# Near products over blocks of 8 in the fifth step, whole bursts and more unread matmuls in the first step of an RWKV-6 and MoE kernel

## The chip, the core and the metric

The kernel runs on one core of a Trainium2 chip. The metric is the device time of an execution in microseconds (us); lower is better. The kernel before was measured at 631.83 us (median of 3; 630.54 to 633.44). Engines: PE (TensorE, matmuls; PEld its weight loads), DVE (VectorE), ACT (ScalarE), POOL (GpSimd), SP (issues DMA).

## The reference

```python
# attention: B=4, H=8, S=768, D=48; per head a D x D state
for t in range(S):
    cur = einsum('bhd,bhe->bhde', u[None] * kt, vt)
    y[:, :, t] = einsum('bhd,bhde->bhe', rt, state + cur)
    state = wt[:, :, :, None] * state + einsum('bhd,bhe->bhde', kt, vt)
# then, on x = y as (3072 tokens, 384):
h = x @ w_in                      # 384 -> 2048
sp = softplus(h)
out = (h * erf(sp)) @ w_out       # 2048 -> 384
```

## The kernel before

Twelve steps, s = 0 to 11, each of 2 x 128 tokens. A step attends (small matmuls and DVE work); the dense layers of earlier steps are laid between as "pieces", so that PE has work while DVE prepares. Inside a half of 64 tokens the products of r and k with their decay are made level by level: blocks of 2 tokens, 4, and so on to 64. Each level is a burst of small matmuls into `pp`, then a scaling of r and k by DVE, on which the next level's burst waits. From s = DIRECT = 4 on, the first four levels are replaced: products of tokens less than 16 apart in a block of 16 are computed element by element ("near products") during the step before, so the step's bursts begin at level 5.

```python
# prepare(s), near products of a block of 16 (cut)
for n in range(1, NEARER):             # NEARER = 5: DVE does distances 0 to 4
    if s == DIRECT and n == NEARER - 1:
        yield
    term(nc.vector, n)                 # terms[n] = r[n:] * k[:16-n]
    carry(nc.vector, n + 1)            # k *= decay
for n in range(1, 4):
    sum_up(n)
for n in range(NEARER, 9):             # GpSimd does the others
    term(nc.gpsimd, n)
    carry(nc.gpsimd, n + 1)
# ... sums over d on DVE, to DRAM and back into the layout of `own`
```

In the first step there are no dense layers to fill PE. Unread matmuls (identity times zeros, results never used) are put there to keep PE's clock up:

```python
# attend(s), one level (cut)
parts = 1 if s else NJ                 # NJ = 2: in step 0 the burst comes in two halves
for part in range(parts):
    for n in range(part * JP // parts, (part + 1) * JP // parts):
        ...                            # 4 small matmuls into pp for each n
    scale(s, level, part, parts)       # DVE
    keep_busy(DM // 2)                 # s == 0 only: one unread matmul of 192 columns
```

The end of a step's attention fades the state on POOL, behind POOL's near products in its queue:

```python
if c:
    nc.gpsimd.tensor_mul(faded[0][:], S[:], ...)                       # L484
...
nc.vector.tensor_add(middle[rows(e)], faded[0][rows(e)], ps[0][...])   # L512, PE's y waits for it
```

Of the kernel before, what the change touches and what calls it, by code (L numbers as in the profile page):

```python
# [15 lines left out]
ALU = mybir.AluOpType  # L16

P = 128
EP = 64
HC = 64  # L20
NC = 2
NJ = 2
# [10 lines left out]



DIRECT = 4
NEAR_LOG = 4
NEARER = 5
NEAR = 1 << NEAR_LOG
LOG = 6  # L40
MASKED = 5


def view(ap, offset, dims):

    return bass.AP(ap.tensor, ap.offset + offset, [ap.ap[0], *dims])
# [12 lines left out]
def kernel(  # L59
# [14 lines left out]
    nc = tc.nc  # L74
    PSUM = bass.MemoryType.PSUM

    n_steps, _, _, JP, C = rkw.shape
    NH, D = v.shape[2:]
    NP = JP // NJ
    NE = NH // JP  # L80
# [51 lines left out]
    def load_step(s, parts=1):  # L132
# [13 lines left out]
        nc.sync.dma_start(out=vt[:], in_=v[s])  # L146
        loaded[s] = t, vt

    rows_of = {}

    def load_rows(s):
# [66 lines left out]
    def rows(e, n=D):  # L218
        return slice(e * EP, e * EP + n)
# [4 lines left out]

    ready = {}

    def scale(s, level, part=0, parts=1):


        in_t, tots = loaded[s][0], ready[s][1]  # L230
        half, nb = 1 << (level - 1), (JP * C >> level) // parts
        halves = view(
            in_t[:, 0:2], half + part * nb * 2 * half,
            [[JP * C - half, 2], [2 * half, nb], [1, half]],
        )
        nc.vector.tensor_mul(  # L236
            halves, halves, view(tots[level - 1], part * nb * 2, [[1, 2], [2, nb], [0, half]])
        )

    def prepare(s):  # L240


        in_t = loaded[s][0]
        if s < DIRECT:
            rk1 = att.tile([P, 2, JP, C], FP32, name="rk1", bufs=1)
            parts = 1 if s else NJ
            def multiply_u(i, x):
                n = slice(i * JP // parts, (i + 1) * JP // parts)
                with_u, plain = (
                    [  # L250
                        t[:, x, n].rearrange("p n (t two) -> p n t two", two=2)[..., one]
                        for t in (rk1, in_t)
                    ]
                    for one in (x, 1 - x)
                )
                if not s and not x:
                    nc.vector.tensor_mul(
                        with_u[0], with_u[1],
                        u_sb[:, :, None].to_broadcast([P, NP, C // 2]),
                    )  # L260
                    nc.vector.tensor_copy(out=plain[0], in_=plain[1])
                    return
                for p in range(NP):
                    of = slice(p, None, NP)
                    nc.scalar.mul(
                        out=with_u[0][:, of], in_=with_u[1][:, of], mul=u_sb[:, p : p + 1]
                    )
                nc.scalar.copy(plain[0], plain[1])

            if s < 2:  # L270
                for i in range(parts):
                    for x in range(2):
                        multiply_u(i, x)
                yield
            else:
                yield
                yield
                multiply_u(0, 0)

        tots, tot = [], in_t[:, 2].rearrange("p n t -> p (n t)")  # L280
        tot_sb = att.tile([P, JP * (C - NC)], FP32, name="tot_sb")
        used = 0
        for level in range(1, LOG + 1):
            tots.append(tot)
            nb = JP * C >> level
            new = tot_sb[:, used : used + nb]
            pair = tot.rearrange("p (n two) -> p n two", two=2)
            nc.gpsimd.tensor_mul(new, pair[:, :, 0], pair[:, :, 1])  # L288
            tot = new
            used += nb  # L290
            if level == 2 and s < DIRECT:
                yield
        if s < DIRECT:
            ready[s] = rk1, tots, tot
            yield
            if s >= 2:
                yield
                multiply_u(0, 1)
            return

        own = att.tile([P, NH, HC], FP32, name="own")
        ready[s] = own, tots, tot
        if s == DIRECT:
            yield

        r, k, w = rows_of.pop(s)
        front = att.tile([P, 2, JP, C], FP32, name="rk1", bufs=1)
        back = wide.tile([P, 2, DM, 2], I32, name="words", bufs=3)
        front = front[:].rearrange("p x n t -> p (x n t)")
        back = back[:].rearrange("p x n two -> p (x n two)").bitcast(FP32)  # L310
        terms = {}

        for room, distances in (
            (front, range(1, 4)), (back, (0, 4)), (front, range(5, 9)), (back, range(9, NEAR))
        ):
            used = 0
            for n in distances:
                size = (NEAR - n) * D
                terms[n] = room[:, used : used + size].rearrange("p (t d) -> p t d", d=D)
                used += size  # L320

        def sum_up(n):
            nc.vector.tensor_reduce(  # L323
                out=view(sums[:], n, [[NEAR + 1, NEAR - n]]), in_=terms[n],
                axis=mybir.AxisListType.X, op=ALU.add,
            )

        def carry(engine, n):

            if 1 < n < NEAR:  # L330
                engine.tensor_mul(  # L331
                    k[:, : NEAR - n], k[:, : NEAR - n], w[:, n - 1 : NEAR - 1]
                )

        def term(engine, n):
            engine.tensor_mul(terms[n], r[:, n:], k[:, : NEAR - n])  # L336

        nc.vector.tensor_mul(terms[0], k, u_row[:, None, :].to_broadcast([P, NEAR, D]))
        for n in range(1, NEARER):
            if s == DIRECT and n == NEARER - 1:  # L340
                yield
            term(nc.vector, n)
            carry(nc.vector, n + 1)
        for n in range(1, 4):
            sum_up(n)
        for n in range(NEARER, 9):
            term(nc.gpsimd, n)
            carry(nc.gpsimd, n + 1)
        if s == DIRECT:
            yield  # L350
        nc.vector.tensor_mul(terms[0], terms[0], r)
        for n in (0, 4):
            sum_up(n)
        for n in range(9, NEAR):
            term(nc.gpsimd, n)
            carry(nc.gpsimd, n + 1)
        yield
        for level in range(1, NEAR_LOG):
            scale(s, level)
        yield  # L360
        for n in range(NEARER, NEAR):
            sum_up(n)
        by_blocks = dram.tile([P, NEAR, NEAR], FP32, name="by_blocks")
        nc.sync.dma_start(out=by_blocks[:], in_=sums[:])
        by_tokens = att.tile([P, NH, NEAR], FP32, name="by_tokens", bufs=1)
        nc.sync.dma_start(
            out=by_tokens[:], in_=by_blocks[:].rearrange("(g b) s t -> (b s) g t", g=NH)
        )
        yield
        scale(s, NEAR_LOG)  # L370
        nb = HC // NEAR
        nc.vector.tensor_mul(
            own[:].rearrange("p n (b t) -> p n b t", t=NEAR),
            block_sb[:, None, :].to_broadcast([P, NH, HC]).rearrange(
                "p n (b t) -> p n b t", t=NEAR
            ),
            by_tokens[:, :, None, :].to_broadcast([P, NH, nb, NEAR]),
        )

    def attend(s, xT, place, behind):  # L380
# [26 lines left out]
                    ps[:], lhsT=ident[:], rhs=in_t[:, 2, :NP], start=True, stop=True  # L407
                )

        for level in range(NEAR_LOG + 1 if s >= DIRECT else 1, LOG + 1):  # L410
            half = 1 << (level - 1)
            rk = made[:] if level == 1 else RK

            pp = products([P, NE, JP, HC])
            m = HC if level <= MASKED else half
            parts = 1 if s else NJ
            for part in range(parts):
                for n in range(part * JP // parts, (part + 1) * JP // parts):
                    for s0 in range(0, C, HC):
                        for e in range(NE):  # L420
                            t0 = s0 if level <= MASKED else s0 + half
                            nc.tensor.matmul(  # L422
                                pp[s0 : s0 + m, e, n, :m],
                                lhsT=rk[rows(e), 1, n, s0 : s0 + m],
                                rhs=rk[rows(e), 0, n, t0 : t0 + m],
                                start=True,
                                stop=True,
                            )
                scale(s, level, part, parts)
                keep_busy(DM // 2)  # L430
            if level == 1 and s == 1:
                stay_warm()
            got = pp[:].rearrange("p e n t -> p (e n) t")
# [214 lines left out]
    def in_order(s, k):  # L648


        for what in ("APPPAPP", "APPPHH", "AHHH", "AHHH")[k]:
            if what == "A":
                advance()
            elif what == "P":
                piece(projs, s - 3)
            else:
                piece(hids, s - 1)
# [170 lines left out]
```

## Time and profile before

| what | before |
|---|---|
| median time | 631.83 us |
| the execution that was profiled | 637.18 us, span 635.4 us |
| PE, DVE, ACT, POOL busy | 97%, 65%, 47%, 44% |
| mean granted PE clock in that execution | 0.981 |

On the profile's page each digit of a row is one of 40 equal slices of the span, in tenths of busy time; in the row PEclk it is the granted clock. "L422 x64" is a group of 64 instruction records of line 422 (an fp32 matmul has two); an arrow in brackets names what ended the idle time before an instruction. Line numbers move by a few between kernels: L422 before is L423 after (the bursts), L606 is L607 (second dense layer), L500 is L501, L484 is L485.

### The profile page before, as it was taken

To read this page: it belongs to the slowest core of one execution; us is meant where nothing else is said; L and a number is where in the kernel's file an instruction comes from. 1 tells how busy PE (TensorE), PEld (TensorE's weight loads), DVE (VectorE), ACT (ScalarE), POOL (GpSimd) and SP (SyncE) were. 2 spreads that over 40 slices of the span, in tenths; PEclk is the share of its full clock that TensorE was granted. 3 is DMA by queue.
4 is the path that set the end of the run, shared out by engine and by line. 5 is a ranking of instruction groups with operands and counts; after the bars stand their busy time and mean duration, and the time that the engine had idled before them with its cause. 6 is when DMAs were issued, how large, how long until landed. Compare 5 with 4: busy or idle time off the path is not lost.

```text
span 635.4 us, 15400 instructions
## 1 busy us (share of the span) xinstructions
PE 619.3 (97%) x6822; PEld 455.2 (72%) x6822; DVE 412.9 (65%) x453; ACT 301.2 (47%) x374; POOL 278.0 (44%) x288
## 2 busy tenths in 40 slices
PE   7989999999799999999999999999999999999997
PEld 6757787578458758758758758758758758768654
DVE  5579498798896797796796797797796430020200
ACT  2446778726534552552552552552553543544600
POOL 4147265549288079079079078078079100000000
PEclk9599999999799999999999999999999999999999
DMA  8167281530600240240240240240220100000000
GB/s 333 78 225 239 103 298 58 203 102 2 200 36 21 52 176 13 63 173 13 59 177 13 69 167 21 58 170 22 44 110 12 26 13 13 7 23 3 1 25 25
DMA packets 32818, 54.82 MB, mean 86 GB/s; under 512 B 19568, under 2 KB 24944, under 8 KB 31344
## 3 DMA queue, kind: packets, MB, share of 16 engines
q1 hardware_dynamic: 31600, 53.25, 24.1%
q8 instruction: 53, 0.87, 0.5%
q10 hardware_dynamic: 1152, 0.59, 0.4%
q14 instruction: 13, 0.11, 0.1%
HBM read 46.88 MB, written 5.77 MB: 83 GB/s over the span
## 4 chain that ended last, share of the span: by engine, by line
PE 84%; DVE 7%; POOL 4%; issue 2%; ACT 2%; DMA 1%; SPq 0%; POOLq 0%; ACTq 0%; DVEq 0%
PE m L606 37%; PE m L583 34%; PE pp L422 5%; PE pp L478 2%; PE y L467 2%; POOL words L331 2%; DVE in L236 2%; PE y L534 1%; PE pp L500 1%; DVE own L441 1%; POOL rk L336 1%; PE y L398 1%; POOL words L336 1%; DMA in<-in_rkw 1%; DVE pp L197 1%
## 5 line engine op out<-in xcount | busy, mean ns | idle before, releaser
L583 PE MATMUL m<-xT,w_in_sb 128*128 128x256 f32 x1152 | 259.5, 382 | 1.5 <-DVE w_in_sb L200 1.3
L606 PE MATMUL m<-w_out_sb,h 128*128 128x384 f32 x768 | 255.7, 492 | 0.1
L583 PEld LDWEIGHTS m<-xT,w_in_sb 128*128 128x128 f32 x1152 | 215.5, 190 | 35.2 <-issue 2.4
L606 PEld LDWEIGHTS m<-w_out_sb,h 128*128 128x128 f32 x768 | 145.1, 191 | 98.7 <-issue 1.8
L236 DVE TENSOR_TENSOR in<-in,tot_sb 128x1024 f32<-128x1024 f32 (+1 forms) x65 | 93.1, 1433 | 42.5 <-PE pp L422 39.8
L592 ACT COPY h<-m 128x512 f32<-128x512 f32 x96 | 56.0, 583 | 133.8 <-PE m L583 133.7
L572 DVE TENSOR_TENSOR h<-h,sp 128x1024 f32<-128x1024 f32 x48 | 73.9, 1579 | 59.6 <-ACT sp L568 59.6
L331 POOL TENSOR_TENSOR words<-words,rest 128x480 f32<-128x480 f32 (+4 forms) x80 | 83.9, 1048 | 6.3
L288 POOL TENSOR_TENSOR tot_sb<-in 128x512 f32<-128x512 f32 x12 | 14.7, 1229 | 120.9 <-DMA in<-in_rkw 120.9
L336 POOL TENSOR_TENSOR rk<-words 128x528 f32<-128x528 f32 (+3 forms) x32 | 54.0, 1688 | 12.7 <-PE pp L422 10.0
L323 DVE TENSOR_REDUCE sums<-words 128x16 f32<-128x768 f32 (+8 forms) x72 | 32.6, 463 | 36.6 <-POOL words L336 36.4
L422 PEld LDWEIGHTS pp<-in 48*64 48x64 f32 (+1 forms) x2304 | 35.9, 135 | 20.1 <-DVE in L236 7.7
L422 PE MATMUL pp<-in 48*64 48x64 f32 (+1 forms) x2304 | 41.1, 223 | 5.7 <-DVE in L236 3.9
L565 ACT ACTIVATE sp<-h 128x2048 f32<-128x2048 f32 x24 | 45.9, 1911 | 0.3
L568 ACT ACTIVATE sp<-sp 128x2048 f32<-128x2048 f32 x24 | 45.9, 1911 | 0.3
L615 ACT COPY o<-m 128x384 f32<-128x384 f32 x24 | 11.5, 478 | 72.8 <-PE m L606 72.6
L568 ACT ACT_TABLE_LOAD x24 | 30.8, 1283 | 18.3 <-issue 18.0
L336 POOL TENSOR_TENSOR words<-words 128x336 f32<-128x336 f32 (+6 forms) x56 | 37.5, 670 | 4.4
L448 ACT COPY own<-pp 32x512 f32<-32x512 f32 x24 | 13.8, 575 | 51.5 <-PE pp L422 51.2
L323 DVE TENSOR_REDUCE sums<-rk 128x15 f32<-128x720 f32 (+6 forms) x56 | 36.7, 712 | 0.0
L288 POOL TENSOR_TENSOR tot_sb<-tot_sb 128x256 f32<-128x256 f32 (+4 forms) x60 | 32.1, 536 | 4.5
L565 ACT ACT_TABLE_LOAD x24 | 30.8, 1283 | 2.3 <-issue 1.9
(66 smaller groups left out, 463.1 us busy)
## 6 DMA issues: line engine op xcount, KB each, us to landing
in<-in_rkw SPq DMA_DIRECT2D x11, 1536.0 KB, 6.5
words<-in_moe_w_in SPq DMA_DIRECT2D x8, 768.0 KB, 5.7
words<-in_moe_w_out SPq DMA_DIRECT2D x8, 768.0 KB, 4.6
words<-in_rk_rows SPq DMA_DIRECT2D x8, 768.0 KB, 8.1
v<-in_v SPq DMA_DIRECT2D x12, 384.0 KB, 6.8
out<-o SPq DMA_DIRECT2D x24, 192.0 KB, 1.9
rest<-in_w_rows SPq DMA_DIRECT2D x8, 384.0 KB, 8.6
in<-in_rkw SPq DMA_DIRECT2D x2, 512.0 KB, 4.4
```

Source lines behind the costliest of these rows:

```text
L236: nc.vector.tensor_mul(halves, halves, view(tots[level - 1], part * nb * 2, [[1, 2], [2, nb], [0, half]]))
L288: nc.gpsimd.tensor_mul(new, pair[:, :, 0], pair[:, :, 1])
L323: nc.vector.tensor_reduce(out=view(sums[:], n, [[NEAR + 1, NEAR - n]]), in_=terms[n], axis=mybir.AxisListType.X, op=ALU.add,)
L331: engine.tensor_mul(k[:, : NEAR - n], k[:, : NEAR - n], w[:, n - 1 : NEAR - 1])
L336: engine.tensor_mul(terms[n], r[:, n:], k[:, : NEAR - n])
L422: nc.tensor.matmul(pp[s0 : s0 + m, e, n, :m], lhsT=rk[rows(e), 1, n, s0 : s0 + m], rhs=rk[rows(e), 0, n, t0 : t0 + m], start=True, stop=True,)
L565: nc.scalar.activation(held[0][:], h[:], AF.Softplus)
L568: nc.scalar.activation(held[0][:], held[0][:], AF.Erf)
L572: nc.vector.tensor_mul(h[:, part], h[:, part], held[0][:, part])
L583: nc.tensor.matmul(ps[:, ff, :], lhsT=w_in_sb[:, g * FG + f + ff, kk * P : (kk + 1) * P], rhs=xT[:, kk, :], start=kk == 0, stop=kk == KT - 1,)
L592: nc.scalar.copy(h[:, f : f + FT, :], ps[:])
L606: nc.tensor.matmul(ps[j][:], lhsT=gs[g][:, f, j * C : (j + 1) * C], rhs=w_out_sb[:, g * FG + f, :], start=g + f == 0, stop=g == NG - 1 and ...
```

## The change

Its intent: at the start of the fifth step PE waits for POOL's near products. With blocks of 8 in that step alone there is less near work, and DVE can do it all; the step then has one more level of matmuls. In the first step, whole bursts and three times 192 unread columns a level, in place of two halves with 192 columns each, are to hold the clock.

```diff
+    def near_log(s):
+        return NEAR_LOG - (s == DIRECT)
...
+        if near < NEAR:                       # s == DIRECT: blocks of 8, DVE alone
+            term(nc.vector, 1, 2, 3)
+            yield
+            term(nc.vector, 4, 5, 6, 7)
+            nc.vector.tensor_mul(terms[0], terms[0], r)
+            yield
+            sum_up(*range(near))
+        else:                                 # as before
...
-        for level in range(NEAR_LOG + 1 if s >= DIRECT else 1, LOG + 1):
+        for level in range(near_log(s) + 1 if s >= DIRECT else 1, LOG + 1):
...
-            parts = 1 if s else NJ
-            for part in range(parts):
-                for n in range(part * JP // parts, (part + 1) * JP // parts):
+            for n in range(JP):
...
-                scale(s, level, part, parts)
-                keep_busy(DM // 2)
+            scale(s, level)
+            keep_busy(DM, DM // 2)
...
-        for what in ("APPPAPP", "APPPHH", "AHHH", "AHHH")[k]:
+        order = ("APPPAPP", "APPPHH", "AHHH", "AHHH")
+        if s == DIRECT:
+            order = ("APPP", "APPP", "APPHH", "AHHH", "AHHH")
+        for what in order[k]:
```

In the last lines P is a piece of the second dense layer (8 records of L606), H one of the first, A a stage of the activation.

More of the change, by code (lines that the diff above doesn't have):

```diff
@@ L37 @@
 NEAR_LOG = 4
-NEARER = 5
 NEAR = 1 << NEAR_LOG
@@ L225, with scale @@
     ready = {}
-    def scale(s, level, part=0, parts=1):
+    def scale(s, level):
         in_t, tots = loaded[s][0], ready[s][1]
-        half, nb = 1 << (level - 1), (JP * C >> level) // parts
-        halves = view(
-            in_t[:, 0:2], half + part * nb * 2 * half,
-            [[JP * C - half, 2], [2 * half, nb], [1, half]],
-        )
+        half, nb = 1 << (level - 1), JP * C >> level
+        halves = view(in_t[:, 0:2], half, [[JP * C - half, 2], [2 * half, nb], [1, half]])
         nc.vector.tensor_mul(
-            halves, halves, view(tots[level - 1], part * nb * 2, [[1, 2], [2, nb], [0, half]])
+            halves, halves, view(tots[level - 1], 0, [[1, 2], [2, nb], [0, half]])
         )
@@ L310, in prepare @@
         back = back[:].rearrange("p x n two -> p (x n two)").bitcast(FP32)
-        terms = {}
+        terms, near = {}, 1 << near_log(s)
+        r, k, w = (x.rearrange("p (q t) d -> p q t d", t=near) for x in (r, k, w))
         for room, distances in (
-            (front, range(1, 4)), (back, (0, 4)), (front, range(5, 9)), (back, range(9, NEAR))
+            ((front, (1, 2, 3, 6, 7)), (back, (0, 4, 5)))
+            if near < NEAR
+            else ((front, (1, 2, 3)), (back, (0, 4)), (front, range(5, 9)), (back, range(9, NEAR)))
         ):
@@ L317, in prepare @@
             for n in distances:
-                size = (NEAR - n) * D
-                terms[n] = room[:, used : used + size].rearrange("p (t d) -> p t d", d=D)
+                size = NEAR // near * (near - n) * D
+                terms[n] = room[:, used : used + size].rearrange(
+                    "p (q t d) -> p q t d", t=near - n, d=D
+                )
                 used += size
-        def sum_up(n):
-            nc.vector.tensor_reduce(
-                out=view(sums[:], n, [[NEAR + 1, NEAR - n]]), in_=terms[n],
-                axis=mybir.AxisListType.X, op=ALU.add,
-            )
@@ L328, in carry @@
-        def carry(engine, n):
-            if 1 < n < NEAR:
-                engine.tensor_mul(
-                    k[:, : NEAR - n], k[:, : NEAR - n], w[:, n - 1 : NEAR - 1]
-                )
-        def term(engine, n):
-            engine.tensor_mul(terms[n], r[:, n:], k[:, : NEAR - n])
-        nc.vector.tensor_mul(terms[0], k, u_row[:, None, :].to_broadcast([P, NEAR, D]))
-        for n in range(1, NEARER):
-            if s == DIRECT and n == NEARER - 1:
-                yield
-            term(nc.vector, n)
-            carry(nc.vector, n + 1)
@@ L344, in prepare, with sum_up @@
-        for n in range(1, 4):
-            sum_up(n)
-        for n in range(NEARER, 9):
-            term(nc.gpsimd, n)
-            carry(nc.gpsimd, n + 1)
-        if s == DIRECT:
-            yield
-        nc.vector.tensor_mul(terms[0], terms[0], r)
-        for n in (0, 4):
-            sum_up(n)
-        for n in range(9, NEAR):
-            term(nc.gpsimd, n)
-            carry(nc.gpsimd, n + 1)
+        def sum_up(*distances):
+            for n in distances:
+                nc.vector.tensor_reduce(
+                    out=view(
+                        sums[:], n, [[near * (NEAR + 1), NEAR // near], [NEAR + 1, near - n]]
+                    ),
+                    in_=terms[n], axis=mybir.AxisListType.X, op=ALU.add,
+                )
@@ new lines, in term @@
+        def term(engine, *distances):
+            for n in distances:
+                engine.tensor_mul(terms[n], r[:, :, n:], k[:, :, : near - n])
+                if n + 1 < near:
+                    engine.tensor_mul(
+                        k[:, :, : near - n - 1], k[:, :, : near - n - 1], w[:, :, n : near - 1]
+                    )
+        u_times = u_row[:, None, None, :].to_broadcast([P, NEAR // near, near, D])
+        nc.vector.tensor_mul(terms[0], k, u_times)
+        if near < NEAR:
+            term(nc.vector, 1, 2, 3)
+            yield
+            term(nc.vector, 4, 5, 6, 7)
[3 more added lines that the diff above has]
+        else:
+            term(nc.vector, 1, 2, 3, 4)
+            sum_up(1, 2, 3)
+            term(nc.gpsimd, 5, 6, 7, 8)
+            nc.vector.tensor_mul(terms[0], terms[0], r)
+            sum_up(0, 4)
+            term(nc.gpsimd, *range(9, NEAR))
@@ L357, in prepare @@
         yield
-        for level in range(1, NEAR_LOG):
+        for level in range(1, near_log(s)):
             scale(s, level)
         yield
-        for n in range(NEARER, NEAR):
-            sum_up(n)
+        if near == NEAR:
+            sum_up(*range(5, NEAR))
         by_blocks = dram.tile([P, NEAR, NEAR], FP32, name="by_blocks")
@@ L369, in prepare @@
         yield
-        scale(s, NEAR_LOG)
+        scale(s, near_log(s))
         nb = HC // NEAR
@@ L415, in attend @@
             m = HC if level <= MASKED else half
-            parts = 1 if s else NJ
-            for part in range(parts):
-                for n in range(part * JP // parts, (part + 1) * JP // parts):
-                    for s0 in range(0, C, HC):
-                        for e in range(NE):
-                            t0 = s0 if level <= MASKED else s0 + half
-                            nc.tensor.matmul(
-                                pp[s0 : s0 + m, e, n, :m],
-                                lhsT=rk[rows(e), 1, n, s0 : s0 + m],
-                                rhs=rk[rows(e), 0, n, t0 : t0 + m],
-                                start=True,
-                                stop=True,
-                            )
-                scale(s, level, part, parts)
-                keep_busy(DM // 2)
+            for n in range(JP):
+                for s0 in range(0, C, HC):
+                    for e in range(NE):
+                        t0 = s0 if level <= MASKED else s0 + half
+                        nc.tensor.matmul(
+                            pp[s0 : s0 + m, e, n, :m],
+                            lhsT=rk[rows(e), 1, n, s0 : s0 + m],
+                            rhs=rk[rows(e), 0, n, t0 : t0 + m],
+                            start=True,
+                            stop=True,
+                        )
+            scale(s, level)
+            keep_busy(DM, DM // 2)
             if level == 1 and s == 1:
```

## The prediction

> **What bounds the kernel now.** I read the engine table first: TensorE (PE) is busy 619 of 635 us, and 71% of the chain that ended last is the two dense layers (L606 37%, L583 34%). From the sixth step (s=5) on, the chain is nothing but PE, at 47.55 us a step (216.43 to 263.98 us), so work done beside PE there cannot matter. What can be won is time in which PE stands idle or runs at a low clock. The second view, the 40 slices, shows where that is: the granted clock dips in slice 2 (16 to 32 us) and in slice 11 (159 to 175 us).
>
> ```profile
> PE   7989999999799999999999999999999999999997
> POOL 4147265549288079079079078078079100000000
> PEclk9599999999799999999999999999999999999999
> ```
>
> The chain of waits in order of time (start, length, what) then shows the passage from the fourth step (s=3) into the fifth (s=4, the first with near products):
>
> ```profile
> 137.43 2.13 POOL words L331
> ...
> 160.24 0.28 POOL words L336
> 160.52 0.80 POOL faded L484
> ...
> 162.56 0.84 POOL faded L516
> ...
> 164.58 1.24 DVE in L236
> 165.86 1.99 PE pp L422 x64
> 167.84 15.07 PE m L606 x40
> ...
> 215.39 1.04 PE y L534 x64
> 216.43 0.93 PE pp L422 x64
> 217.36 13.10 PE m L606 x40
> ```
>
> GpSimd (POOL) computes the far near products in 21 instructions from 136.01 to 160.52 us; the state's fading (L484) queues behind them, VectorE (DVE) waits for that, and PE waits for DVE. Two costs can be read off against the next step. An undisturbed passage is y (215.39) to pp (216.43), 1.04 us; here y starts at 160.04 (PE's timeline) and pp at 165.86, so 4.78 us are lost waiting. Then pp and the first 40 matmuls take 17.05 us against 14.03: 3.02 us lost to a half clock. Sum 7.8 us.
>
> For the first dip I asked for stretches of 3.4 us (columns: length, then busy time and instructions of PE, PEld, DVE, ACT and POOL; granted clock; DMA) and for ACT's instructions:
>
> ```profile
> 8.00:11.40 3.40, 3.29 (x102) 2.56 (x102) 2.68 (x4) 1.27 (x5) 3.05 (x4) 1.00 1.03 424
> 11.40:14.80 3.40, 2.13 (x68) 1.41 (x66) 2.58 (x4) 0.00 (x0) 0.51 (x3) 1.00 1.07 433
> ...
> 18.20:21.60 3.40, 3.40 (x68) 2.63 (x64) 1.40 (x3) 1.76 (x5) 1.66 (x2) 0.50 0.25 94
> ```
>
> ```profile
> 19.84 1.31 ACT L265 ACTIVATE rk<-in,u_sb 128x128 f32<-128x128 f32 x4 [10.57 <-DMA in<-in_rkw]
> ...
> 28.38 1.18 ACT L448 COPY own<-pp 32x512 f32<-32x512 f32 x2 [4.93 <-PE pp L422]
> ```
>
> Split to 0.2 us, the clock is half from 14.77 to 31.8 us. The reader should see that it fell after a stretch with PE busy 2.13 of 3.4 us, and that full busyness with small matmuls (3.40 us of 18.2 to 21.6) did not bring it back.
>
> **What the Trainium skill says.** "TensorE: Matmul & The Clock Gate", section "What's actually happening": the clock is full or half, decided over free-running windows of 3413 ns. The trace agrees: the changes at 14.77, 31.8, 164.97 and 171.79 us lie 5, 39 and 2 such windows apart. The page speaks of an idle window; here the clock fell with no PE gap above 0.98 us, so the threshold for partly busy windows is my guess. "GPSIMD Engine Reference", section "3.1 Elementwise — side-by-side cycle accounting": about 2.6 cycles an element on GpSimd against 1 on VectorE. The trace: POOL products of 240 and 48 elements take 0.70 and 0.29 us, 2.1 ns an element; DVE reductions of the same sizes 0.40 and 0.20 us, 1.04 ns. The same page, section "1. Specifications": GpSimd shares SBUF interfaces with two-input VectorE instructions. The trace: a pair of h products takes 3.76 us at 149.54, with POOL busy, and 2.35 us at 166.86, with POOL idle.
>
> **Part one: blocks of 8 for s=4.** DVE now does 15 products of 6240 elements in all (768 twice, 2688 of r times k, 2016 of decay) and 8 reductions of 3456. From its timeline a product costs n x 1.04 ns + 0.2 us start to start, a reduction n x 1.04 ns + 0.1: 9.5 + 4.4 = 13.9 us. Before, DVE itself had 10 products of 6528 elements and 16 reductions of 6528: 8.8 + 8.4 = 17.2 us. So even DVE's load falls, and POOL's 24.5 us vanish with the contention. Run through step 3 in the new order: the first products at 124.84 as before, scale of level 4 at 131.2 (was 131.84), level 5 at 136.7 (137.26), the sums until 143, level 6 then (141.93 before; PE first needs it at 147.14, so it is hidden). POOL fades the state early; DVE's first sum with L500's result comes at 154.2, right behind PE; the second fading ends about 156.4, S_next at 157.6, the last scale at 158.8. PE finds it done and begins s=4 at 161.08 with no wait, at full clock. All 7.8 us are recovered.
>
> Added: level 4 of s=4 on PE, 64 matmul records, 0.93 us by the row at 216.43, plus about 0.05. Its mask copy (0.7 us on DVE) lies beside PE.
>
> Moved: the order of pieces in s=4 puts 24 matmuls of L606 (7.9 us) ahead of level 5, at which the near products of s=5 are prepared. So POOL's chain for s=5 starts later within the step: pp of level 5 at 169.9, DVE's products from 172.7, POOL from 181.1 to 204.7 (23.6 us, as at 229.48 to 253.04), fading until 205.5. PE ends L500 at 200.2 and, 10.3 us after L500's start at 199.3, wants level 5 of s=5 at 209.6. DVE needs from 205.6: two sums with the fading between, 3.2 us, and the scale, 1.2: 210.0. That is a new wait of about 0.5 us, once; s=6 is back in slack. Net of part one: 7.8 - 0.95 - 0.5 = 6.35 us.
>
> **Part two: the first step.** Before, the halves of a burst wait on each other (pp at 12.67 waits 0.98 us for the scale of the other half), giving 4.0 us a level at half clock. Now a level is burst 1.05, scale 1.22, hand-overs 0.2: 2.45 us at full clock, and the unread matmuls (192 columns take 0.53 us, 384 some 0.86) fill PE for 2.4 of it. Level 2 begins at about 11.5, level 3 at 14.5, level 6 at 21.9. But ACT multiplies by u for the second step from 19.84, when its DMA lands, until 23.45, ahead of the copy of level 6: so `own` is ready at 24.6, not 29.56. Behind it the rest of the step loses its slow part too; ACT (level 6 copy, 1.8 us of weight conversion, kT copy) sets kT at 27.4, and L500 starts at 27.5 instead of 33.39. Steps 1 and 2 wait only for on-chip work (no wait for DMA in their lists), so the 5.9 us carry through.
>
> If the clock falls all the same, a level is PE-bound: burst 2.1 and unread 1.58 + 0.94, 4.6 us against 4.0 before. Level 6 comes near 28.4, L500 near 36.4: 3 us lost.
>
> **Rivals.**
> 1. Full clock kept: 631.8 - 6.35 - 5.9 = 619.6 us. For it: by my model PE is busy some 80% of the windows at 7.9 and 11.4 us, and almost all of later ones, against the 63% that failed; and the full-width share is 28 to 38%, against some 14% in the failing window and 25% in the one before, which held.
> 2. Clock lost in step 0: 631.8 - 6.35 + 3 = 628.5. For it: the windows run free, so single executions can differ, and in the old slow phase unread matmuls made up a third of PE's streaming without bringing the clock back. I give it one in four.
> 3. The POOL chain of s=5 becomes a bigger wait than 0.5 us, being late by 9 us in its step. Against: after L500 there are still 8 us of dense matmuls before PE needs the result. For: contention can stretch POOL's products (1.80 against 1.20 us for the same kind). It would cost 1 to 3 us: 621 to 623.
> 4. DVE becomes the bound in step 3 since it does all near products: against, its load falls by 3.3 us; worth nothing.
>
> **Range and chances.** The first rival's sum, 619.6, lies on the 2% border (619.2). Rivals 2 and 3 both pull up; little pulls down but a smaller contention than assumed (1 to 2 us). I take 620.8, with 617 to 628.5 for the range: faster by over 2% 0.31, within 2% 0.68, slower 0.01.
>
> **What would show it.** No PE wait before pp at the start of s=4 and no clock dip in slice 11; 21 fewer POOL instructions (267 of 288); kT's copy ending near 27.4 and the clock at full between 10 and 27 us, else the second rival; L500 of s=4 about 37 us after level 5; a PE wait on DVE's scale of about half a microsecond at the start of s=5, with POOL's `faded` behind it. It is wrong if the clock falls in step 0, or if that last wait is several us.

## The result

The changed kernel takes 628.38 us (median of 4; 628.27 to 628.51) against 631.85 us (median of 4), both correct. The ratio is 0.9944, with a 95% interval of 0.9921 to 0.9967: the same within 2%. Ratios here are the mean time of one kernel's fast runs over the mean of the other's in the same rounds, so not quite the ratio of the medians. I had predicted 620.8 us. The range was not left by the measured value (617 to 628.5), but only because it held the case of a lost clock, and the clock was not lost. The gain is 3.5 us where I forecast 11: the prediction was wrong.

The profile after, the same three rows of the page:

```profile
PE   8989999999999999999999999999999999999997
POOL 4448184600278197096097097097087100000000
PEclk9999999999999999999999999999999999999999
```

Both dips of the clock are gone. PE is busy 611.9 of 626.6 us. The chain of waits through the passage into the fifth step, and on to the sixth:

```profile
156.31 1.04 PE y L535 x64
157.35 0.93 PE pp L423 x64
158.28 7.94 PE m L607 x24
...
202.03 0.80 POOL faded L485
204.07 0.84 POOL faded L517
206.09 1.24 DVE in L235
207.37 1.16 PE pp L423 x64
```

The passage into the fifth step is 1.04 us, as in an undisturbed step. The wait on POOL's fading has moved to the start of the sixth step, where the bursts begin at 207.37.

The first step, ACT's and PE's rows that answer to those of before:

```profile
24.25 1.17 ACT L449 COPY own<-pp 32x512 f32<-32x512 f32 x2 [0.44 <-PE pp L423]
...
27.28 1.01 ACT L483 COPY kT<-pp 128x1024 f32<-128x1024 f32 x1
```

```profile
28.35 0.94 PE L501 MATMUL m<-v,kT 64*48 64x48 f32 x64 [0.34 <-ACT kT L483]
```

L501 begins at 28.35, where I had put 27.5. Its counterpart in the profile of before:

```profile
33.39 0.94 PE L500 MATMUL m<-v,kT 64*48 64x48 f32 x64 [0.24 <-ACT kT L482]
```

So from profile to profile the spans shrink by 8.8 us (635.4 to 626.6), two and a half times what the medians show (3.5). That gap was the first thing to explain: either the profiled execution of before was not a typical one, or its profile cost it 5 us that the kernel after did not pay.

### The profile page after: what moved, and what is told of

The parts are those of the page before. It is cut to its first block, busy times and chain, and to the rows that moved or that the text cites. A ratio compares the mean times of both kernels' runs of the same rounds, so it can differ in the third digit from the quotient of the medians.

```text
span 626.6 us, 15491 instructions
## 1 busy us (share of the span) xinstructions
PE 611.9 (98%) x6886; PEld 451.0 (72%) x6886; DVE 402.6 (64%) x445; ACT 301.3 (48%) x374; POOL 258.0 (41%) x267
## 4 chain that ended last, share of the span: by engine, by line
PE 83%; DVE 8%; POOL 3%; issue 2%; ACT 2%; DMA 1%; SPq 0%; DVEq 0%; POOLq 0%; ACTq 0%
PE m L607 36%; PE m L584 34%; PE pp L423 5%; DVE in L235 3%; PE pp L479 2%; PE y L468 2%; PE y L535 2%; PE pp L501 1%; PE m L686 1%; DMA in<-in_rkw 1%; DVE sums L328 1%; POOL tot_sb L287 1%; DVE h L573 1%; DVE own L442 1%; DVE words L340 1%
## 5 line engine op out<-in xcount | busy, mean ns | idle before, releaser
L235 DVE TENSOR_TENSOR in<-in,tot_sb 128x1024 f32<-128x1024 f32 x60 | 90.8, 1514 | 41.2 <-PE pp L423 39.1
L573 DVE TENSOR_TENSOR h<-h,sp 128x1024 f32<-128x1024 f32 x48 | 70.8, 1516 | 60.7 <-ACT sp L569 60.7
L340 POOL TENSOR_TENSOR words<-words,rest 128x480 f32<-128x480 f32 (+4 forms) x70 | 72.4, 1035 | 5.5
L328 DVE TENSOR_REDUCE sums<-words 128x6 f32<-128x288 f32 (+8 forms) x66 | 30.4, 472 | 35.6 <-POOL words L338 35.3
L338 POOL TENSOR_TENSOR rk<-words 128x528 f32<-128x528 f32 (+3 forms) x28 | 47.9, 1712 | 6.2 <-issue 4.0
L423 PEld LDWEIGHTS pp<-in 48*64 48x64 f32 (+1 forms) x2368 | 33.8, 125 | 17.4 <-issue 8.0
L423 PE MATMUL pp<-in 48*64 48x64 f32 (+1 forms) x2368 | 38.4, 212 | 4.8 <-DVE in L235 2.2
L287 POOL TENSOR_TENSOR tot_sb<-tot_sb 128x256 f32<-128x256 f32 (+4 forms) x60 | 35.1, 584 | 4.5
L328 DVE TENSOR_REDUCE sums<-rk 128x14 f32<-128x672 f32 (+9 forms) x54 | 34.7, 698 | 0.0
L338 POOL TENSOR_TENSOR words<-words 128x336 f32<-128x336 f32 (+6 forms) x49 | 31.6, 646 | 3.8
```

The lines of the kernel that those rows point to most:

```text
L235: nc.vector.tensor_mul(halves, halves, view(tots[level - 1], 0, [[1, 2], [2, nb], [0, half]]))
L287: nc.gpsimd.tensor_mul(new, pair[:, :, 0], pair[:, :, 1])
L328: nc.vector.tensor_reduce(out=view(sums[:], n, [[near * (NEAR + 1), NEAR // near], [NEAR + 1, near - n]]), in_=terms[n], axis=mybir.AxisLi ...
L338: engine.tensor_mul(terms[n], r[:, :, n:], k[:, :, : near - n])
L340: engine.tensor_mul(k[:, :, : near - n - 1], k[:, :, : near - n - 1], w[:, :, n : near - 1])
L423: nc.tensor.matmul(pp[s0 : s0 + m, e, n, :m], lhsT=rk[rows(e), 1, n, s0 : s0 + m], rhs=rk[rows(e), 0, n, t0 : t0 + m], start=True, stop=True,)
```

## The experiments

Each run comes with the time and mean clock of every execution, and with executions of the kernel before on the same chip. All kernels gave correct results.

The runs come from several jobs. `before_again`, `step0_only`, `near8_only` and `whole_old_unread` ran in one (chip 2); `step0_filled`, `convert_first`, `level5_early` and `both_fixes` in another (chip 6), and the three looks in a third (chip 14). The kernel after was timed with the result only, four times. Executions of before at a clock of 1.000 took 629.67 and 629.82 us in the first of these jobs and 628.79 to 629.07 in the second, so medians of different jobs compare to some 0.8 us at best; where a difference of that size matters below, I go to the profiles.

### before_again: the kernel before, five more rounds

No edit.

> The kernel before, unchanged. Theory (profile not typical): the profiled execution of before, 637.2 us, lost the clock in the first step for longer than its timed executions of 631.9 us do. Then the executions of this run differ by several us and the slower ones have the lower mean clock: about 0.987 or more at 631.9 us, against 0.981 at 637.2. Rival (same clock, the profile cost 5 us): every execution has a clock near 0.981 whatever its time, and the 5 us are found outside the first step.

Measured: 632.57 us (median of 6). Its executions and the 11 of the kernel before that ran beside it:

```
this    636.97 (0.981)  631.47 (0.995)  631.65 (0.995)  637.53 (0.981)  633.25 (0.995)  631.89 (0.995)
before  637.71 (0.981)  629.82 (1.000)  633.09 (0.995)  632.14 (0.995)  629.67 (1.000)  637.48 (0.981)
        637.52 (0.981)  632.06 (0.995)  631.49 (0.997)  631.97 (0.995)  637.48 (0.981)
```

The time of the kernel before goes by the clock. Over the 32 executions of it in these jobs for which the clock is listed (the profiled one of 637.18 us, also at 0.981, is not counted):

| mean clock | executions | mean time |
|---|---|---|
| 0.981 | 7 | 637.4 us |
| 0.989 | 2 | 635.1 us |
| 0.995 | 14 | 632.3 us |
| 0.997 | 4 | 631.0 us |
| 1.000 | 5 | 629.2 us |

The profile that I predicted from is of the slowest pattern, one execution in five; the median lies in the pattern of 0.995. The rival (the profile's own cost) falls: 637.5 us comes with 0.981 and never with another clock.

### before_look1, before_look2, before_look3: single profiles of the kernel before

No edit.

> Kernel before, one profile more, in the hope of a typical execution (clock 0.995, some 632 us). Theory: such a profile shows a half clock for 6.8 us from about 160 us and none in the first step, whose L500 then starts near 29 us and not at 33.4. Rival: the step starts as late as in the profile shown, and the time differs elsewhere.

> As before_look1: each execution falls by chance into one of the clock's patterns, so I take a second look.

> As before_look1, a third look. If one of the three shows clock 1.000 (some 629.5 us): no half clock anywhere, and the waits before pp in the passage are still there.

Measured: 635.01, 631.33 and 635.24 us, at clocks 0.989, 0.997 and 0.989. None fell into 0.995 or 1.000, but the second lies within 0.5 us of the median and has no half clock in the first step. Its PE rows (start, length, what):

```profile
29.30 0.94 PE L500 MATMUL m<-v,kT 64*48 64x48 f32 x64 [0.35 <-ACT kT L482]
```

```profile
123.23 1.56 PE L606 MATMUL m<-w_out_sb,h 128*128 128x384 f32 x4 [1.37 <-POOL w_out_sb L204]
...
157.19 0.66 PE L534 MATMUL y<-in,s 48*48 48x64 f32 x32
157.68 0.86 PE L534 MATMUL y<-in,middle 48*48 48x64 f32 x32
161.20 1.94 PE L422 MATMUL pp<-in 48*64 48x64 f32 x64 [2.67 <-DVE in L236]
...
210.38 1.11 PE L422 MATMUL pp<-in 48*64 48x64 f32 x64
```

Four things are to be seen. With a full clock the old first step brings L500 to 29.30, only 0.95 us later than the new one, as the theory had it. In the fourth step PE waits 1.37 us for weights still being converted on POOL; it waits 1.33 us at this place in the profile after too, so that wait is no product of the change, but in the profile that I used it was only some 0.4 us (16 records took 5.82 us there instead of 5.43). Because PE comes later here, its wait in the passage is shorter: y to pp takes 4.01 us (157.19 to 161.20), which is 3.1 above the 0.93 that the same two rows of after are apart (156.24 and 157.17), not 4.8. And the half clock lasts 3.4 us (161.3 to 164.7), not 6.8. The first look's half clock was at 22.4 to 32.6 and 165.7 to 169.2 us, the third's at 22.7 to 33.0 and 166.1 to 169.5: the pattern changes from execution to execution.

That wait for weights shows a second way in which my profile was not typical. In it POOL's first decay total took 1.04 us, and the two products of the activation that DVE made at that time (L572) took 3.53; in `before_again` it was 3.13 and 2.37:

```profile
117.65 1.04 POOL L288 TENSOR_TENSOR tot_sb<-in 128x512 f32<-128x512 f32 x1 [3.55 <-DMA in<-in_rkw]
```

```profile
117.93 3.13 POOL L288 TENSOR_TENSOR tot_sb<-in 128x512 f32<-128x512 f32 x1 [3.83 <-DMA in<-in_rkw]
```

All other profiles of before, and those of `step0_only` and `step0_filled`, are like `before_again`: POOL 2.74 to 3.25 us, DVE 2.35 to 2.38, then a PE wait of 1.4 us for the weights, and 4.0 to 4.1 us from y to pp in the passage (`step0_filled` has its unread matmuls there). The 5.82 us that I predicted from occur once, and not by the clock: `before_again` has the same clock, 0.981, and 4.00 us.

### step0_only: the change of the first step alone

```diff
-            parts = 1 if s else NJ
+            parts = 1
...
-                keep_busy(DM // 2)
+                keep_busy(DM, DM // 2)
```

> Kernel before plus the change of the first step alone (whole bursts, 384 and 192 unread columns). My prediction on record says 5.9 us gained, the two profiles say 5.0 (L500 at 28.35 against 33.39). Theory (profile not typical): against the typical before only 0 to 2 us are gained, 630 to 632 us. Rival (typical before loses as much): 626 to 627 us.

Measured: 630.93 us (630.39 to 632.72), ratio to before 0.9968 (0.9923 to 1.0013), clocks 0.992 to 0.997. The theory's 0 to 2 us holds; the 5.9 us of my prediction do not appear. None of the 6 executions is near 637 us, which alone could be chance; but over all six kernels with the new first step and its added columns (this one, after, and the four of the last job) it is none of 34, with no clock below 0.992 and no time above 632.72, against 7 at 0.981 in the 32 of before. So the edit removes the executions of 637 us. Its profile keeps the wait and the lost clock of the passage.

### near8_only: the first step as before, blocks of 8 in the fifth

The edit, against the kernel after, cut (`scale` gets its parts back too):

```diff
-            for n in range(JP):
-                ...
-            scale(s, level)
-            keep_busy(DM, DM // 2)
+            parts = 1 if s else NJ
+            for part in range(parts):
+                ...
+                scale(s, level, part, parts)
+                keep_busy(DM // 2)
```

> Kernel after with the first step as before: blocks of 8 in the fifth step alone. Prediction on record: 6.35 us gained. The profile after shows two waits that I put too low, 1.3 us in the fourth step (weights of the second layer) and 1.2 us at the start of the sixth: theory, 4 to 5 us gained against a before that loses the clock at this place, so near 627.5 us, with the clock of the first step still varying between executions. Rival (the passage costs less in a typical before): 1 to 3 us gained, 629 to 631.

Measured: 628.51 us (627.86 to 635.1), ratio 0.9943 (0.9885 to 1.0001). Five executions have clock 1.000 and lie between 627.86 and 629.55, as fast as the whole change (628.38); one has 0.984 and 635.1 (no profile shows where). The patterns of 0.995 and 0.997, 18 of the 32 of before, do not occur in these six, so with the old first step they come from the passage. And with a full clock the edit of the first step is worth nothing that these executions show; only the profiled one, the slowest of the five, is 1.2 us behind the profile of after. My 4 to 5 us "against a before that loses the clock" came out at 3.6 by the medians, below the theory and above the rival's 1 to 3.

### whole_old_unread: the kernel after with the old amount of unread columns

```diff
-            keep_busy(DM, DM // 2)
+            keep_busy(DM // 2, DM // 2)
```

> Kernel after with the old amount of unread matmuls in the first step (192 and 192 columns) but whole bursts. If it is the unread columns that hold the clock, it falls again in the first step (mean clock 0.975 to 0.99, 629 to 633 us, with spread); if the whole bursts do it, the clock stays at 0.999 and the time at 628.4 or less.

Measured: 628.68 us (627.65 to 630.41), clocks 0.999, 0.997, 0.992, 0.995, 0.997 and 0.995. Neither expectation fits whole. The clock is below 0.999 in five of six executions; of the 22 with the same whole bursts and the added columns (after, `convert_first`, `level5_early`, `both_fixes`) 19 are at 0.999 or 1.000. So in whole bursts it is the added columns that, as a rule, hold the clock. That is not shown for halves: `near8_only` has halves and the old columns, and five of its six are at 1.000. Where the clock dropped here is not shown either, as the profiled execution is the one at 0.999. But whole bursts with the old columns kept it at 0.992 or more, and the mean time is within a microsecond of after's; one execution with a clock of 0.995 took only 627.65 us, less than any of after. That the unread columns cost path time themselves would explain it, but was only argued.

### step0_filled: the clock of the passage held, the wait left

To `step0_only`, unread matmuls where PE waits in the passage:

```diff
+        if s == DIRECT - 1:
+            stay_warm(3)              # three unread matmuls of 512 columns
```

> Kernel before with the new first step and three unread 512-column matmuls in the passage from the fourth to the fifth step, where PE waits 2.7 us: the clock held, the wait left. Theory (in the passage the typical before loses some 2 us by the clock, and the change's net gain beyond that is about 1.4 us): clock 0.999 in all executions, 629.2 to 629.9 us, against 630.9 without the filling and 628.4 of after. Rival (the wait itself is what the change gained): no faster than 630.9.

Measured: 629.05 us (628.71 to 631.17), clock 1.000 in four of six and 0.997 in two, where I had expected 0.999 in all. The PE rows of the passage:

```profile
157.38 2.84 PE L406 MATMUL m<-in,ident 128*128 128x512 f32 x6
160.15 1.16 PE L422 MATMUL pp<-in 48*64 48x64 f32 x64
161.25 13.17 PE L609 MATMUL m<-w_out_sb,h 128*128 128x384 f32 x40
```

The burst still begins at 160.15 (160.24 in step0_only), but at full clock: it and its 40 matmuls end 1.7 us sooner. This prices the clock of the passage at 1.9 us by the medians (630.93 to 629.05) and 1.7 by the two profiles (630.40 to 628.71), and leaves 0.7 or 0.4 us (629.05 to 628.38; profiles 628.71 to 628.35) for everything else that the near products over blocks of 8 do. The medians are of three jobs, but the rows bear them out. The rival falls.

### convert_first, level5_early and both_fixes: the two waits left in the kernel after

`convert_first` moves the last conversion of weights ahead, so that on POOL it does not stand behind the decay totals, which wait for a DMA:

```diff
-        ("js", "j"),
+        ("jsj",),
```

> Kernel after, with the last conversion of weights moved one place earlier in the fourth step, so that on GpSimd it no longer stands behind the decay totals that wait for a DMA. In the profile after, PE waits 1.3 us for it. Theory (this wait is on the path): 1.2 us faster than after's 628.4, so 627.2, and no PE wait on GpSimd's w_out_sb. Rival (the wait only hides the next one): 628.4.

Measured: 626.86 us (626.62 to 626.98), clock 1.000 in all six, ratio to before 0.9926. That is 1.5 us below after, and the PE wait on w_out_sb is gone from the list of waits. The profiles agree: L501 starts at 28.39 (28.35 in after), y of the passage at 154.68 (156.24). The theory holds.

`level5_early` has one piece ahead of level 5 in the fifth step, not three:

```diff
-            order = ("APPP", "APPP", "APPHH", "AHHH", "AHHH")
+            order = ("AP", "APPPPP", "APPHH", "AHHH", "AHHH")
```

> Kernel after, with one piece of the projection instead of three before level 5 of the fifth step and five instead of three after it, so that the near products of the sixth step start 5.2 us earlier. Theory (their lateness on GpSimd makes the PE wait of 1.18 us at the start of the sixth step): the wait goes, 627.2 us. Rival (DVE is the bound there, not GpSimd's chain): the wait stays, 628.4.

Measured: 627.01 us (625.28 to 628.42), clock 1.000 in four and 0.997 in two. PE's start of the sixth step:

```profile
204.89 0.67 PE L535 MATMUL y<-in,s 48*48 48x64 f32 x32
205.38 0.63 PE L535 MATMUL y<-in,middle 48*48 48x64 f32 x32
205.82 1.11 PE L423 MATMUL pp<-in 48*64 48x64 f32 x64
```

There is no wait before pp: the rows follow one another as in every later step. By the medians this is 1.4 us. The time of the profiled execution alone would not show it: there L501 starts 1.33 us later than in after (29.68), and the wait of 1.33 us for the weights is missing, as in the profile that I predicted from (POOL's first decay total 1.24 us, DVE's products 3.25). The rows do, and so does `both_fixes` against `convert_first`, below. The theory holds. Two executions lost the clock for one window all the same; in the profiled one it was from 16.7 to 20.1 us, in the first step. So the change makes that loss rare but does not exclude it.

`both_fixes` has both edits.

> Both edits on the kernel after. If the two waits add: 628.4 - 1.3 - 1.2 = 625.9 us, faster than both kernels. If one hides behind the other: 627.2.

Measured: 625.45 us (625.2 to 627.35), ratio 0.9908 (0.987 to 0.9946), clock 1.000 in five of six. The two add up: 628.38 - 1.5 - 1.4 = 625.5. Against `convert_first` in the same job it is 1.4 us, and y to pp at the start of the sixth step takes 0.93 us where `convert_first` has 2.30. It beats both kernels, and it is 6.3 us below the median of before in the same rounds (631.71).

## Why the prediction was wrong

The mechanism was right in each part. The base and four sizes were off. For a like-for-like sum I take the second look at before (631.33 us) and the profile after (628.35 us), which differ by 2.98 us. From pp at the start of s=4 to pp at the start of s=5 is 49.18 us in the look. The step after it, undisturbed, takes 47.55, so 1.63 are the clock's loss. In after it is 50.20: 2.65 us more than 47.55, of which 1.37 are the new wait; the rest is put down to the added level. All measured terms are from the timeline of PE. (My 4.78 and 3.02 set timeline starts against starts of the chain, which lie some 0.1 to 0.2 us later; from the timeline alone that profile gives 4.89 and 2.84.)

| term | predicted, us | measured, us | from |
|---|---|---|---|
| first step | -5.9 | -0.95 | L500 at 29.30, L501 at 28.35 |
| wait in the passage | -4.78 | -3.08 | y to pp 4.01, after 0.93 |
| clock in the passage | -3.02 | -1.63 | pp to pp 49.18 instead of 47.55 |
| added level, with its breaks | +0.95 | +1.28 | 2.65 less 1.37 |
| new wait in s=5 | +0.5 | +1.37 | y to pp 2.30 instead of 0.93 |
| sum | -12.25 | -3.01 | |

**The step that failed: "So `own` is ready at 24.6, not 29.56 ... L500 starts at 27.5 instead of 33.39."** The 33.39 is a number of one execution, the profiled one of 637.18 us, and I took its gain off the median of 631.8. The new first step went almost as I worked it out: the copy of level 6 ran from 24.25 to 25.42 and kT's from 27.28 to 28.29, where I had 24.6 and 27.4 for their ends; the start-up burst of identity matmuls ended 1.4 us later than in the profile that I used (7.53 us long, not 6.08). But most executions of before (23 of the 32 have a clock of 0.995 or more) lose no clock in the first step, and the one of them that a profile shows reaches L500 at 29.30. About 5 of the 5.9 us were never in the median. Even the 0.95 us that are left are a difference of two profiles; the executions of `near8_only` at full clock do not show them. The spread of before, 630.54 to 633.44, did not show its slow pattern at all, and the profiled time beside it was a warning of 5.35 us that I did not use.

**"If the clock falls all the same": my second rival did not come.** I feared for the clock of the new step. After's executions hold it at 0.999 or 1.000; `whole_old_unread` shows that in whole bursts the added columns do that, and `level5_early` that they do not do it always. My reason for it was only half right: I had PE busy in almost all of the later windows, and in the profile after it is busy 2.48, 2.84 and 3.06 us of the three stretches of 3.4 us from 14.77 us on. The "full-width shares" of 14% and 25% I cannot get back from the trace either: by busy time the unread matmuls fill 0.93 and 1.44 of 3.41 us there, 27% and 42%. What the new first step buys is the end of the 637 us executions of before, which a median hardly shows. In the mean it is an estimated 1.3 us: of the 32 executions 7 lie 5.1 us and 2 lie 2.8 us above the row of 0.995.

**"All 7.8 us are recovered": true of that profile, 4.8 of a typical execution.** The wait is what POOL's chain ends later than PE arrives. Against the look my profile has L500 4.09 us later, PE's arrival (y) only 2.85, as PE had not waited for the converted weights, and the end of POOL's chain 4.65. So 1.24 of the 1.8 us by which its wait is longer are the missing wait for the weights; the other 0.6 lie in the near products, which, counted from L500, began 1.0 us later, after DVE's slower products of the activation. The clock was half for 6.8 us in my profile, for 3.4 in the look. No profile caught the commonest pattern, 0.995; 0.5% of 630 us is an estimated 6.3 us at half clock, which would fit the passage alone, and the difference of 1.3 us between the rows 0.995 and 0.997 of the table is what the look lacks of it. `step0_filled` separates them on the chip: without the clock's loss, the wait that is removed and the work that is added nearly cancel (0.4 to 0.7 us).

**"That is a new wait of about 0.5 us, once": the right wait, mis-sized.** It measured 1.18 us by its row and 1.37 from y to pp. POOL's chain for s=5 ran as long as I said, 23.65 us (178.38 to 202.03), but I had put its start 11.2 us after level 5's burst (169.9 to 181.1), and it came 12.2 us after (166.15 to 178.38). From DVE's first product to POOL's first it took 9.25 us (169.13 to 178.38) where I had 8.4 (172.7 to 181.1). POOL's decay totals ran beside DVE's products from 168.23 to 174.33, and the first two took 1.18 and 1.31 us; in before, a step later and with POOL idle, the same two took 0.95 and 0.90 (219.30 and 220.16). `level5_early` removes the wait by starting the chain sooner, which confirms its cause. My list of marks also had a slip: it puts L500 "about 37 us after level 5"; my own numbers give 29.4, and 29.6 was measured.

**Right as put:** DVE did not become the bound in the fourth step (fourth rival); 21 POOL instructions went (288 to 267); the sixth step onward runs as before.

Left open: inside the bursts of the first step PE pauses 0.3 to 1.2 us where the profile names no wait ("issue"), in several profiles of whole bursts; no run was made on it. The 40 records of identity matmuls at the very start take 6.08 to 7.59 us in different profiles, all shown with a clock of 1.00, and no run shows why. Nor is it shown what decides which of POOL and DVE is the slower one at the decay totals of the fourth step, or which busy share of a window decides the clock.

## What to carry to other kernels

Before adding up gains from a profile, hold the time of the profiled execution against the median and look at the clock of every execution: a profile is one draw, and a loss that it shows is worth its share of all executions only. Where a chain on a slow engine sets a wait, a piece of work put ahead of its start can come back as a wait one step later (here 1.37 us, gone when two pieces were moved behind). Unread matmuls can keep a clock up: in the first step they narrowed the spread, which a median hardly shows; in the passage, where most executions lost the clock, they were worth 1.7 to 1.9 us.

## What the Trainium skill lacked or had wrong

- "TensorE: Matmul & The Clock Gate", section "What's actually happening", speaks of an idle window; in the profile of before the clock fell after a window with PE busy 2.13 of 3.4 us and no gap above 0.98 us. The page has no threshold for partly busy windows. Nor did a stretch with PE busy for all of its 3.40 us (18.2 to 21.6 us, small matmuls and unread ones) bring the clock back.
- The same section says that the ramp penalty is under 1% of a typical kernel. That is the start alone, and no run here contradicts it; but with the later losses the patterns of the clock spread one unchanged kernel over 628.79 to 637.71 us, 1.4%, so they cannot be left out of a prediction of this size.
- That section speaks of a start that varies from run to run. That losses in the middle of a kernel come and go too, so that a single profile can be untypical (637.18 us against a median of 631.83), stands on neither that page nor "Perfetto Trace Analysis".
